# Four of sixteen row tiles of block A's qkv projection are taken out of the projection phase and computed inside block B's attention loop

## The chip, the cores and the metric

The kernel runs on one core of one Trainium2 chip. The metric is the device time of one execution in microseconds (us), and the change is judged by the median over repeated runs. TensorE is called PE here, VectorE DVE, ScalarE ACT, GpSimd POOL and SyncE SP, as in the profile; PEld is PE's loading of weights.

## What is computed

Two attention blocks, A and B, each on an input of 2048 rows and 640 columns with 32 heads of 20 columns. Their outputs stand side by side in the result. All arrays are 32-bit floats.

```python
def _A_ref(x, wqkv, wo):               # W, dil = 8, 2
    q, k, v = qkv[0], qkv[1], qkv[2]   # x @ wqkv, cut into heads
    idx = pos[:, None] - off[None, :]  # 8 positions, 2 apart, backwards
    mask = idx >= 0
    logits = jnp.einsum("bhsd,bhswd->bhsw", q, kg) * scale
    logits = jnp.where(mask[None, None, :, :], logits, -1e9)
    attn = _softmax(logits, axis=-1)
    o = jnp.einsum("bhsw,bhswd->bhsd", attn, vg)
    return (lambda x, *d: x.transpose(*d))(o, 0, 2, 1, 3).reshape(B, S, D) @ wo

def _B_ref(x, wqkv, wo):               # full attention
    scores = jnp.einsum("bhqd,bhkd->bhqk", q, k) * (Dh ** -0.5)
    p = _softmax(scores, axis=-1)
    o = jnp.einsum("bhqk,bhkd->bhqd", p, v)
    return (lambda x, *d: x.transpose(*d))(o, 0, 2, 1, 3).reshape(B, S, D) @ wo
```

## The kernel before

Products of full precision are made from three matmuls: each operand is cut into a rounded part and a remainder (`split`, line 173), and `PASSES` (line 31) names the three pairs of parts that are multiplied. A projection of 128 rows is therefore 5 chunks of the 640 inputs times 3 pairs, that is 15 matmuls into one PSUM bank (`rows15`, line 264; `a_rows`, line 270).

The program has four stretches, each running into the next.

1. **Block A's qkv projection** (lines 515 to 555). Four passes over the 1920 output columns, of 512, 384, 512 and 512 columns (`AC`). In each pass 16 row tiles of 128 rows are projected one after another. ACT copies each tile's PSUM bank into a buffer `ro` (three buffers under the tag `ao`), and SP stores it in DRAM (`a_store`, line 277: `qa_d`, `ka_d`, `va_d`). The weights of the next pass are loaded and split in the middle of a pass (`a_pieces`, line 241).
2. **Block B's q and k projection** (from line 597): 40 groups of 15 matmuls, 512 columns each, stored to `qb_d` and `kb_d`. Block A's attention, which is POOL's work, begins here.
3. **Block B's v projection** (`v_group`, line 926): 32 groups of 15 matmuls of 320 columns, and with them the first 24 steps of the maxima.
4. **Block B's attention loop** (from line 1008), 512 steps. 16 steps make a unit: four heads (a group, 8 in all) times 512 query rows (four to a group), so there are 32 units. A step has two score tiles of two heads each. The exponent needs a row maximum before it, so each score is computed twice: once with the queries along the partitions, for the maximum (DVE, `mx`), and once with the keys along the partitions, for the exponent (ACT, `e`). The maxima run 24 steps ahead of the exponents (`LEAD`). The row maxima go through DRAM (`max_rows`, line 636: `mdr`) and come back as two further rows of the query stack `bq`, so that the score matmul subtracts them.

PE's order in the loop is written out by hand. `UNIT` (near line 847) is the table of one unit, and `b_units` (line 853) walks it. Its entries are: `P`, a step of probabilities times values (16 to a unit, eight matmuls in groups of 32 columns); `ss`, two score matmuls for ACT, in two PSUM banks; `MM`, two matmuls for maxima, reduced together by one DVE instruction over 1024 columns; `sm`, one of each, whose maximum is a DVE instruction over 512 columns; and `G`, which is block A's output projection for half a row tile (`a_out`, line 504), together with the small DVE instructions that have been put aside (`flush`). PSUM has eight banks, and `one` and `two` (lines 142 and 148) choose the bank that will be free first by a running estimate. `UNIT` holds 16 `P`, 18 `ss`, 18 `MM`, 28 `sm` and one `G`.

In this loop POOL does block A's attention (`a_attention`, line 446), paced at one piece in four steps, and adds up the outputs (`braw`). SP issues all transfers in program order. In the first unit of each group it loads the keys, queries and values of the next group (`b_pieces`, line 563): the key stack `bk` is one tile and the query stack `bq` another, of four quarters, out of a pool of four large tiles with the tag `big`. Before the loop the same four hold the columns of x.

In the trace the two kinds of matmuls are told apart by their operands: `ps_st<-bq,bk` with 62 rows is a score for ACT, `ps_st<-bk,bq` with 60 rows a score for a maximum, `ps_st<-e,vb` probabilities times values, `ps_st<-ww,aot` block A's output projection. Nearly all instructions carry line 60, that of the helper which emits them.

Of the kernel before, what the change touches and what calls it, by code (L numbers as in the profile page):

```python
# [40 lines left out]
NKB = 16  # L41
NS = NG * NQC * NKB
# [22 lines left out]
def attention_pair(ctx, tc, xa, wqk_a, wv_a, wo_a, xb, wqk_b, wv_b, wo_b, oa, ob):  # L65
# [98 lines left out]
    va_d = dr.tile([2, PAD + HS, D], F32, name="va_d")  # L164
    qb_d = dr.tile([4, 2 * DH, H, 512], F32, name="qb_d")
# [21 lines left out]
    def columns(n):  # L187

        return (sb.tile([128, 2, KC - 1, 512], F32R, tag="big", bufs=4, name="xn"),
                sb.tile([128, 2, 1, 512], F32R, tag=f"last{n % 4 // 2}", bufs=2, name="xl"))  # L190
# [4 lines left out]
    def x_pieces(x, n, second=None):  # L195

        t = columns(n)
# [106 lines left out]
    XA = [columns(0)]  # L304
# [5 lines left out]
    t, more = x_pieces(xa, 1)  # L310
# [5 lines left out]
    loads = []  # L316
    for n in (2, 3):
        t, more = x_pieces(xa, n)
        XA.append(t)
        loads += more  # L320
# [29 lines left out]
    def a_fetch(n):  # L350
        if n >= len(UNITS):
            return
        t, c = UNITS[n]
        hf, r0 = divmod(t * 128, HS)
# [166 lines left out]
    for k in range(KC):  # L521
        for c in PASSES:
            for t in range(4):
                a_rows(first[t], XA[0], 0, t, W, (k,), (c,))
    for n in range(NA):
        nxt = None
        for t in range(NT):
# [7 lines left out]
            if loads and (n == 0 or t % 2):  # L535
                loads.pop(0)()
            if n == 0 and t == 12:
# [5 lines left out]
            if n + 1 < NA and t == (6 if n == 0 else 2):  # L543
                nxt, loads = a_pieces(n + 1)
            if n == NA - 1:
# [4 lines left out]
                if t % 4 == 0 and t:  # L550
                    w, more = x_pieces(xb, t // 4 - 1)
                    XB.append(w)
# [8 lines left out]
    stacks = {}  # L561

    def b_pieces(g):
        k = sb.tile([128, 2, S], F32R, tag="big", bufs=4, name="bk")
        q = sb.tile([128, NQC, 2, 512], F32R, tag="big", bufs=4, name="bq")
        v = sb.tile([128, NKB, VG], F32, tag="vb", bufs=2, name="vb")
        stacks[g] = (q, k, v)
        out = []
        hs = [slice(g * GH + 2 * r, g * GH + 2 * r + 2) for r in range(2)]

        def add(t, src, runs):
            for r0, s0, n in runs:
                out.append(lambda: sp.dma_start(t[r0:r0 + n].bitcast(F32), src[s0:s0 + n]))
        for r in range(2):
            for r0, s0, n in BK_RUNS:
                add(k[r * HALF:], kb_d[:, hs[r]], [(r0, s0, n)])
        for qc in range(NQC):
            for r in range(2):
                for r0, s0, n in BQ_RUNS:
                    add(q[r * HALF:, qc], qb_d[qc, :, hs[r]], [(r0, s0, n)])  # L580
        return out[:4], out[4:]

    def v_piece(g, b0, b1):

        sp.dma_start(stacks[g][2][:, b0:b1], vb_d[b0 * 128:b1 * 128, g * GH * VC:g * GH * VC + VG]
# [9 lines left out]
    for m in range(0, 10, 2):  # L595
        nxt = []
        for n in range(4):
            for j in range(2):
# [25 lines left out]
                if m == 8 and n > 1:  # L624
                    if (n, j) == (2, 0):
                        k_loads, q_loads = b_pieces(0)
# [81 lines left out]
    def m_matmul(i, j, r, p):  # L708
# [3 lines left out]
        q, k, v = stacks[g]  # L712
# [7 lines left out]
    def max_end(i, n=2):  # L720
# [3 lines left out]
        if left_m[u] == 0:  # L724
            max_rows(*mxt[u], stacks[u // NQC][0], u % NQC)
# [15 lines left out]
    def s_matmul(i, pl, r, p):  # L741
        u, kb = divmod(i, NKB)
        g, qc = divmod(u, NQC)
        q, k, v = stacks[g]
# [26 lines left out]
    def b_pv(i):  # L771
# [15 lines left out]
        for j in range(GH):  # L787
            pe.matmul(acc[32 * j:32 * j + 32, :], stacks[g][2][:, kb, j * VC:j * VC + 32], P[i][j % 2][:, j // 2],
# [21 lines left out]
    def b_two(what):  # L810
# [39 lines left out]
        "MM sm ss P MM MM ss P ss MM sm sm").split()  # L850
    SLOT = UNIT[:UNIT.index("G")].count("P") - 1

    def b_units(pv, group):
# [5 lines left out]
        for i in range(0, NS - LEAD, NKB):  # L859
            for t in UNIT if i + NKB <= NS - LEAD else PAIR * (NKB // 4):  # L860
# [3 lines left out]
                elif t == "G":  # L864
                    group()
                elif t == "ss":
# [20 lines left out]
    def out_first(qc):  # L887

        o = columns(2)
# [54 lines left out]

    V_GROUPS = [(n, half, s) for n in (2, 3, 0, 1) for half in range(2) for s in range(4 * n, 4 * n + 4)]
# [156 lines left out]
```

## Time and profile before

| What | Value |
|---|---|
| median of 3 runs | 1775.66 us |
| lowest and highest | 1774.33 and 1777.3 us |
| the profiled execution | 1773.91 us |
| its span, from the first to the last instruction | 1772.1 us |
| matmuls | 11,211 |
| block A's projection on PE | 5.3 to 212.2 us |
| block B's q and k projection | 212.2 to 349.0 us |
| block B's v projection | 349.0 to 442.9 us |
| the loop's units 0 to 30, by the first score of each | from 439.5 us on |
| granted clock of PE | 1.00 throughout |

The profile is that of one execution. Its page has the busy time of each engine, the span in 40 slices, the transfer queues, the chain of work that ended last, and the costliest groups of instructions. Two cautions apply. A matmul's end is modelled, so PE counts as busy while its results are on the way. And a duration in a group's row is that of one instruction from start to end; in a train, the next may start a little before the last has ended. In a timeline, the bracket behind a row holds the idle time ahead of it on that engine and what ended it.

### The profile page before, as it was taken

What the parts mean: (1) busy time and instruction counts of PE and PEld (TensorE: products, weight loads), DVE (VectorE), ACT (ScalarE), POOL (GpSimd) and SP (SyncE); (2) the same over time, 40 slices, a digit from 0 to 9 for tenths busy, and PEclk for the clock granted to TensorE, in tenths of its full rate; (3) what the DMA queues carried; (4) which work ended last, traced back from release to release, by engine and by line L of the source; (5) the groups of instructions that cost most, each with busy time, mean ns of one, the idle gap of its engine ahead of it and who ended that gap; (6) DMA issues with size and microseconds to landing.
All of it is one profiled execution on the core that took longest, in us unless ns stands there. A gap on an engine that the chain in (4) does not pass through costs nothing.

```text
span 1772.1 us, 31387 instructions
## 1 busy us (share of the span) xinstructions
PE 1761.4 (99%) x11211; PEld 982.3 (55%) x11211; DVE 1332.0 (75%) x1774; ACT 1325.7 (75%) x2593; POOL 1218.8 (69%) x1072
## 2 busy tenths in 40 slices
PE   9999999999999999999999999999999999999999
PEld 8988888888444444444444444444444444444569
DVE  3100232267999999999999999999999999999400
ACT  4222322222999999999999999999999999998981
POOL 0000058448698988989898898989898898745442
PEclk9999999999999999999999999999999999999999
DMA  6333596876443534364444435353543534222123
GB/s 230 112 98 110 175 309 244 278 227 200 121 123 114 138 103 129 115 164 113 129 114 140 119 97 149 123 144 105 156 129 93 143 103 120 87 63 62 57 70 115
DMA packets 191188, 240.20 MB, mean 136 GB/s; under 512 B 89020, under 2 KB 115260, under 8 KB 190040
## 3 DMA queue, kind: packets, MB, share of 16 engines
q1 hardware_dynamic: 190456, 237.54, 44.7%
q8 instruction: 88, 1.44, 0.3%
q14 instruction: 68, 0.56, 0.1%
q10 hardware_dynamic: 576, 0.66, 0.1%
HBM read 173.21 MB, written 64.91 MB: 134 GB/s over the span
## 4 chain that ended last, share of the span: by engine, by line
PE 86%; DVE 5%; ACT 3%; POOL 3%; DMA 1%; issue 1%; SPq 1%; POOLq 0%; DVEq 0%; ACTq 0%
PE ps_st L60 86%; DVE mx L60 5%; ACT e L60 2%; POOL akv L60 1%; ACT more L60 1%; POOL braw L60 1%; SPq L60 1%; DMA bq<-qb_d 1%; DMA stg<-wv_b 0%; ACT al L60 0%; DMA back<-tr_d 0%; POOL aot L60 0%; DMA tr_d<-turn 0%; POOL al L60 0%; POOL ao L60 0%
## 5 line engine op out<-in xcount | busy, mean ns | idle before, releaser
L60 DVE TENSOR_REDUCE mx<-ps_st 128x2 f32<-128x1024 f32 (+1 forms) x1452 | 1204.3, 901 | 53.6 <-PE ps_st L60 50.6
L60 ACT ACTIVATE e<-ps_st 128x512 f32<-128x512 f32 x2048 | 1062.2, 612 | 54.2 <-PE ps_st L60 41.7
L60 PE MATMUL ps_st<-bq,bk 62*128 62x512 f32 x2048 | 616.9, 445 | 1.4 <-ACT e L60 0.9
L60 PEld LDWEIGHTS ps_st<-bq,bk 62*128 62x128 f32 x2048 | 284.1, 184 | 492.6 <-ACT e L60 372.4
L60 PE MATMUL ps_st<-bk,bq 60*128 60x512 f32 x2048 | 551.4, 434 | 2.6 <-DMA bq<-qb_d 1.0
L60 PE MATMUL ps_st<-e,vb 128*32 128x512 f32 x4096 | 542.9, 604 | 0.2
L60 POOL TENSOR_TENSOR braw<-braw,more 128x512 f32<-128x512 f32 x224 | 288.0, 1286 | 147.9 <-ACT more L60 131.8
L60 POOL TENSOR_TENSOR akv<-akv,aq 128x1280 f32<-128x1280 f32 x64 | 188.2, 2940 | 234.8 <-DMA akv<-ka_d 234.7
L60 POOL TENSOR_TENSOR akv<-akv 128x640 f32<-128x640 f32 (+3 forms) x304 | 281.8, 927 | 23.8
L60 PEld LDWEIGHTS ps_st<-bk,bq 60*128 60x128 f32 x2048 | 257.0, 184 | 53.9 <-ACT e L60 25.2
L60 ACT COPY ro<-ps_st 128x320 f32<-128x320 f32 (+2 forms) x124 | 61.3, 496 | 198.9 <-PE ps_st L60 150.8
L60 PEld LDWEIGHTS ps_st<-e,vb 128*32 128x32 f32 x4096 | 82.0, 108 | 154.4 <-issue 74.1
L60 POOL TENSOR_TENSOR akv<-akv,al 128x1280 f32<-128x1280 f32 x64 | 152.1, 2377 | 0.2
L60 PE MATMUL ps_st<-wc,xn 128*128 128x512 f32 (+1 forms) x576 | 134.0, 378 | 0.0
L60 ACT COPY more<-ps_st 128x512 f32<-128x512 f32 x224 | 132.5, 592 | 1.8 <-PE ps_st L60 1.4
L60 PE MATMUL ps_st<-ww,xn 128*128 128x320 f32 x768 | 125.7, 314 | 0.0
L60 PEld LDWEIGHTS ps_st<-ww,xn 128*128 128x128 f32 x768 | 113.4, 188 | 20.0 <-ACT ve L60 8.4
L60 PEld LDWEIGHTS ps_st<-wc,xn 128*128 128x128 f32 x576 | 106.9, 189 | 17.6
L60 PE MATMUL ps_st<-xn,w 128*128 128x512 f32 x480 | 115.8, 390 | 0.0
L60 PEld LDWEIGHTS ps_st<-xn,w 128*128 128x128 f32 x480 | 90.1, 188 | 19.4
L60 ACT CAST pr<-ps_st 128x512 fp32r<-128x512 f32 x40 | 23.5, 587 | 101.4 <-PE ps_st L60 101.4
L60 DVE TENSOR_TENSOR pr<-ps_st,pr 128x512 fp32r<-128x512 f32 x40 | 27.7, 691 | 91.7 <-ACT pr L60 91.7
(64 smaller groups left out, 985.3 us busy)
## 6 DMA issues: line engine op xcount, KB each, us to landing
akv<-ka_d SPq DMA_DIRECT2D x128, 320.0 KB
akv<-va_d SPq DMA_DIRECT2D x128, 320.0 KB
kb_d<-pr SPq DMA_DIRECT2D x20, 512.0 KB
qb_d<-pr SPq DMA_DIRECT2D x20, 512.0 KB
bk<-kb_d SPq DMA_DIRECT2D x16, 640.0 KB
bq<-qb_d SPq DMA_DIRECT2D x64, 160.0 KB
rb<-s_d SPq DMA_DIRECT2D x128, 64.0 KB
stg<-xb SPq DMA_DIRECT2D x12, 512.0 KB
```

The lines of the kernel that those rows point to most:

```text
L60: return self.tc.keep_in_program_order(op(*a, **k))
```

## The change

`UP = 12`: the projection phase now has 12 row tiles in each of its four passes. The last four row tiles are projected in the loop, 320 columns in each of units 0 to 23 (four tiles times six parts of the 1920 columns).

- At tile 9 of each pass, `a_keep` stores the split weights of the pass in DRAM (`wa_d`, six parts of 1.6 MB).
- In the loop, `a_load` brings one part back into the large tile `big2`, which holds nothing else then (`wx`). `a_more`, called at the new entry `V` of the table, does 15 matmuls of 320 columns, an ACT copy and a store, and has the next `a_load` issued three steps later. At the first part of a row tile, `a_columns` loads the tile's 128 rows of x, which POOL splits.
- Units 0 to 23 use a new table, `UNIT_V`, with 16 `P`, 16 `ss`, 16 `MM`, 32 `sm`, one `G` and one `V`. It has the entry `V` behind its fourth `P`. Units 24 to 31 keep `UNIT`.
- The four large tiles now have fixed homes. The keys alternate between `big0` and `big3`. The queries of all groups share one tile in `big1`, a ring of four quarters: in steps 1, 3, 5 and 7 of each unit (from unit 1) the quarter of the unit three later is loaded into the place of the quarter just finished. The last query chunks' x columns, and those of the output projection at the end, get their homes by a list.
- The first chunk of block B's x is loaded in the last pass but one, since `big0` is free.

```diff
+UP = 12
...
+    wa_d = dr.tile([6, 128, 2, KC, 320], F32, name="wa_d")
...
+    def big(home, shape, name):
+
+        return sb.tile(shape, F32R, tag=f"big{home}", bufs=1, name=name)
...
-        return (sb.tile([128, 2, KC - 1, 512], F32R, tag="big", bufs=4, name="xn"),
+        return (big(n if home is None else home, [128, 2, KC - 1, 512], "xn"),
...
+    def a_keep(g, W):
+
+        c, end = AC[g], AC[g + 1]
+        while c < end:
+            m, c1 = divmod(c, 320)
+            n = min(320 - c1, end - c)
+            for wi in range(2):
+                for half, (a, b) in enumerate(AK):
+                    sp.dma_start(wa_d[m, :, wi, a:b, c1:c1 + n],
+                                 W[wi][half][:, :, c - AC[g]:c - AC[g] + n].bitcast(F32))
+            c += n
...
-        for t in range(NT):
+        for t in range(UP):
...
+            if t == 9:
+                a_keep(n, W)
+            if n == NA - 2 and t == 7:
+                w, more = x_pieces(xb, 0)
+                XB.append(w)
+                loads += more
...
+    def b_keys(g):
+        k = big(3 * (g % 2), [128, 2, S], "bk")
+        stacks[g] = (k, v)
+        return [lambda r=r, r0=r0, s0=s0, n=n: sp.dma_start(
+            k[r * HALF + r0:r * HALF + r0 + n].bitcast(F32), kb_d[s0:s0 + n, g * GH + 2 * r:g * GH + 2 * r + 2])
+            for r in range(2) for r0, s0, n in BK_RUNS]
+
+    def b_queries(g, qc):
+
+        return [lambda r=r, r0=r0, s0=s0, n=n: sp.dma_start(
+            rings[0][r * HALF + r0:r * HALF + r0 + n, qc].bitcast(F32),
+            qb_d[qc, s0:s0 + n, g * GH + 2 * r:g * GH + 2 * r + 2])
+            for r in range(2) for r0, s0, n in BQ_RUNS]
...
+            for t in UNIT_V if i // NKB < 6 * (NT - UP) else UNIT if i + NKB <= NS - LEAD else PAIR * (NKB // 4):
...
+                elif t == "V":
+                    more()
...
+    UNIT_V = (
+        "sm P sm MM ss P sm ss MM sm P ss MM sm P sm sm MM sm V sm ss MM sm P sm MM ss P sm MM sm ss P sm MM "
...
+    rows_a = [(t, m) for t in range(UP, NT) for m in range(6)]
+    xt, wt = [], []
+    in_dram = [UP]
+
+    def a_columns(t):
+
+        u = sb.tile([128, 640], F32, tag="stg", bufs=3, name="stg")
+        raw = u.rearrange("p (k c) -> p k c", c=128)
+        sp.dma_start(raw, xa[:, t * 128:(t + 1) * 128].rearrange("(k p) c -> p k c", p=128))
+        x = (sb.tile([128, 2, KC - 1, 128], F32R, tag="last1", bufs=2, name="xn"),
+             sb.tile([128, 2, 1, 128], F32R, tag="x5", bufs=2, name="xl"))
+
+        def parts():
+            for u, r in zip(x, (raw[:, :KC - 1], raw[:, KC - 1:])):
+                gp.tensor_copy(u[:, 0], r)
+                gp.tensor_tensor(u[:, 1], r, u[:, 0].bitcast(F32), ALU.subtract)
+            xt.append(x)
+        after(5, parts)
+
+    def a_load():
+
+        if not rows_a:
+            return
+        t, m = rows_a[0]
+        if m == 0:
+            a_columns(t)
+        w = big(2, [128, 2, KC, 320], "wx")
+        sp.dma_start(w.bitcast(F32), wa_d[m])
+        wt.append(w)
+
+    def a_more():
+
+        t, m = rows_a.pop(0)
+        if m == 0 and len(xt) > 1:
+            xt.pop(0)
+        x, w = xt[0], wt.pop(0)
+        p = bank()
+        rows15(p, lambda xi, k: chunk(x, xi, k), [w[:, 0], w[:, 1]])
+        hf, r0 = divmod(t * 128, HS)
+        pad = PAD if m > 1 else 0
+        store_rows(p, (qa_d, ka_d, va_d)[m // 2][hf, pad + r0:pad + r0 + 128, m % 2 * 320:m % 2 * 320 + 320])
+        if m == 5:
+            after(2, in_dram.__setitem__, 0, t + 1)
+        after(3, a_load)
...
+        if groups == 26:
+            a_load()
...
-            k_loads, q_loads = b_pieces(g + 1)
-            for n, fn in enumerate(k_loads + q_loads + [lambda g=g + 1: v_piece(g, 0, NKB)]):
+            for n, fn in enumerate(b_keys(g + 1)):
                 after(1 + 2 * n, fn)
+            after(41, v_piece, g + 1, 0, NKB)
+        if i >= NKB and i % NKB in (1, 3, 5, 7) and i // NKB + 3 < NG * NQC:
+            b_queries(*divmod(i // NKB + 3, NQC))[i % NKB // 2]()
```

PE's order in the second unit, at its fourth `P` (`ps_st<-e,vb`), before; `bq,bk` is a score for ACT and `bk,bq` one for DVE:

```order
L60 MATMUL ps_st<-bq,bk 128x512 x2
L60 MATMUL ps_st<-bk,bq 128x512 x2
L60 MATMUL ps_st<-bq,bk 128x512
L60 MATMUL ps_st<-bk,bq 128x512
L60 MATMUL ps_st<-e,vb 32x512 x4
L60 MATMUL ps_st<-bq,bk 128x512
L60 MATMUL ps_st<-bk,bq 128x512 x3
L60 MATMUL ps_st<-bq,bk 128x512 x3
L60 MATMUL ps_st<-bk,bq 128x512
L60 MATMUL ps_st<-bq,bk 128x512
```

The same place now. `wx` are the weight parts from DRAM, `xn` and `xl` the two kinds of parts of the row tile's x:

```order
L61 MATMUL ps_st<-e,vb 32x512 x4
L61 MATMUL ps_st<-bq,bk 128x512
L61 MATMUL ps_st<-bk,bq 128x512
L61 MATMUL ps_st<-bq,bk 128x512
L61 MATMUL ps_st<-bk,bq 128x512 x3
L61 MATMUL ps_st<-bq,bk 128x512
L61 MATMUL ps_st<-bk,bq 128x512
L61 MATMUL ps_st<-wx,xn 128x320 x12
L61 MATMUL ps_st<-wx,xl 128x320 x3
L61 MATMUL ps_st<-bq,bk 128x512
L61 MATMUL ps_st<-bk,bq 128x512
L61 MATMUL ps_st<-bq,bk 128x512 x2
```

The fourth `P` was followed by five pairs and the next `P`; it is now followed by four pairs, three of which are `sm` and one `MM`, then by the 15 matmuls of `V`, and then by further pairs ahead of the next `P`.

SP's order in the second unit of the loop (the one that starts at 480.7 us in the trace of before), from `G` on; `mdr` are the row maxima on their way through DRAM, `akv` block A's keys or values, `tr_d` and `back` the way of block A's output through DRAM:

```order
L60 DMA s_d<-sm 128x16
L60 DMA rb<-s_d 32x512 x4
L60 DMA mdr<-mtr 16x2x32 x4
L60 DMA tr_d<-turn 128x640
L60 DMA akv<-va_d 128x640 x2
L60 DMA bq<-qb_d 20x1024
L60 DMA bq<-mdr 2x1024 x2
L60 DMA bq<-qb_d 40x1024
L60 DMA back<-tr_d 32x20x32 x4
L60 DMA akv<-va_d 128x640 x2
L60 DMA bq<-qb_d 20x1024
L60 DMA ot_b<-braw 20x512 x4
```

The same unit now, from the issue of `wx` on:

```order
L61 DMA wx<-wa_d 128x3200
L61 DMA bq<-qb_d 40x1024
L61 DMA akv<-va_d 128x640 x2
L61 DMA oa<-ro 128x320
L61 DMA s_d<-sm 128x16
L61 DMA rb<-s_d 32x512 x4
L61 DMA mdr<-mtr 16x2x32 x4
L61 DMA tr_d<-turn 128x640
L61 DMA akv<-va_d 128x640 x2
L61 DMA bq<-mdr 2x1024 x2
L61 DMA back<-tr_d 32x20x32 x4
```

The pieces of `bq` from `qb_d` stood between the stores of `mdr` and behind its way back; they now stand ahead of `s_d<-sm`, in the first half of the unit, with `wx` (1.6 MB) among them, six entries ahead of the stores of `mdr`.

69 lines of the change are left out of this document (27 added, 42 removed).

## The prediction

> **What bounds the kernel now.** I read the page first, then the busy time of the engines in chosen stretches, then the timelines of single engines in one unit of the loop.
>
> ```profile
> span 1772.1 us, 31387 instructions
> PE   9999999999999999999999999999999999999999
> PEld 8988888888444444444444444444444444444569
> DVE  3100232267999999999999999999999999999400
> GB/s 230 112 98 110 175 309 244 278 227 200 121 123 114 138 103 129 115 164 113 129 114 140 119 97 149 123 144 105 156 129 93 143 103 120 87 63 62 57 70 115
> ```
>
> PE is marked full in every slice, but this hides two regimes. In the first ten slices PEld is at eight to nine tenths and DVE low; from the eleventh PEld falls to four tenths and DVE is full. The stretches say the same in numbers (columns: length, then PE, PEld, DVE, ACT and POOL busy, clock, transfer share, GB/s); the first three are passes 2, 3 and 4 of block A's projection, the others lie in the loop:
>
> ```profile
> 61.03:102.69 41.66, 41.66 (x242) 41.66 (x240) 3.67 (x8) 10.65 (x24) 0.00 (x0) 1.00 0.35 110
> 102.69:157.46 54.77, 54.77 (x242) 45.09 (x241) 3.46 (x5) 11.87 (x21) 0.00 (x0) 1.00 0.31 100
> 157.46:212.23 54.77, 54.77 (x241) 45.09 (x240) 7.93 (x8) 15.46 (x24) 0.00 (x0) 1.00 0.46 151
> 700.00:800.00 100.00, 99.58 (x685) 43.52 (x683) 97.37 (x131) 93.29 (x185) 89.33 (x78) 1.00 0.47 133
> 900.00:1000.00 100.00, 99.77 (x686) 43.72 (x685) 98.11 (x137) 93.25 (x185) 91.46 (x81) 1.00 0.50 138
> ```
>
> The projection is PE's alone: nothing else is near full, and the chain of waits has one unbroken piece of PE there:
>
> ```profile
> 1.36 344.40 PE ps_st L60 x1564
> ```
>
> In the loop DVE is the fullest, with about 2% idle, ACT has 7% and POOL 9 to 11%. How full PE really is has to be read from a timeline. First two steps without `G` (start, length), and PEld's row for the waits inside them:
>
> ```profile
> 732.92 0.49 PE L60 MATMUL ps_st<-bq,bk 62*128 62x512 f32 x2
> ...
> 733.83 1.07 PE L60 MATMUL ps_st<-e,vb 128*32 128x512 f32 x8
> 734.82 0.50 PE L60 MATMUL ps_st<-bq,bk 62*128 62x512 f32 x1
> ...
> 736.64 1.07 PE L60 MATMUL ps_st<-e,vb 128*32 128x512 f32 x8
> 737.64 0.51 PE L60 MATMUL ps_st<-bq,bk 62*128 62x512 f32 x2
> ```
>
> ```profile
> 735.57 0.18 PEld L60 LDWEIGHTS ps_st<-bq,bk 62*128 62x128 f32 x1 [0.22 <-DVE mx L60]
> ...
> 736.15 0.18 PEld L60 LDWEIGHTS ps_st<-bq,bk 62*128 62x128 f32 x1 [0.32 <-ACT e L60]
> ```
>
> Two steps take 737.64 - 732.92 = 4.72 us. Of these PE waits 0.22 + 0.32 = 0.54 us for banks that DVE and ACT still read. Eight such double steps make a unit, so PE waits about 8 x 0.54 = 4.3 us in a unit, a tenth of it. That is all the room that new work has on PE.
>
> **The change part by part.** What goes: tiles 12 to 15 of each of the four passes. Three passes are of 512 columns and one of 384. By the stretches a tile is 54.77 / 16 = 3.42 us or 41.66 / 16 = 2.60 us. Twelve of the first and four of the second make 41.1 + 10.4 = **51.5 us**, all on the path, since PE runs through. The first pass loses the same four tiles at its end, and I give them the same 3.42 us. A rule of the Trainium skill speaks against this term: "TensorE: Matmul & The Clock Gate", section "Back-to-back issue gap", gives about 131 ns for each 512-column matmul in a sustained stream. By it 15 would take 1.97 us, the sixteen tiles at most 31.5 us, and the forecast below would be some 20 us later. The stretches have 3.42 us, and the measurement decides.
>
> What comes: 24 entries `V`. Their price c, per unit, is the question. What the trace has of the kind is `G`, the same 15 matmuls of 320 columns:
>
> ```profile
> 740.86 2.47 PE L60 MATMUL ps_st<-ww,aot 128*128 128x320 f32 x15
> 743.26 0.50 PE L60 MATMUL ps_st<-bq,bk 62*128 62x512 f32 x1
> ...
> 1535.56 2.47 PE L60 MATMUL ps_st<-ww,aot 128*128 128x320 f32 x15
> ...
> 1575.19 4.64 PE L60 MATMUL ps_st<-ww,aot 128*128 128x320 f32 x30
> 1579.76 0.49 PE L60 MATMUL ps_st<-bq,bk 62*128 62x512 f32 x1
> ...
> 1617.06 4.64 PE L60 MATMUL ps_st<-ww,aot 128*128 128x320 f32 x30
> ```
>
> The upper bound is in these rows. From 1535.56 to 1575.19 a unit with one half tile in `G` takes 39.63 us. From 1575.19 to 1617.06, with two directly behind each other, it takes 41.87 us. The second set holds PE for (1579.76 - 1575.19) - (743.26 - 740.86) = 2.17 us, and the unit grew by 2.24: nothing was hidden. The lower bound comes from DVE's rows, the busiest engine:
>
> ```profile
> L60 DVE TENSOR_REDUCE mx<-ps_st 128x2 f32<-128x1024 f32 x596 | 718.5, 1217 | 27.7 <-PE ps_st L60 26.8
> L60 DVE TENSOR_REDUCE mx<-ps_st 128x1 f32<-128x512 f32 x856 | 553.0, 681 | 25.9 <-PE ps_st L60 23.8
> L60 ACT COPY ro<-ps_st 128x320 f32<-128x320 f32 x60 | 25.6, 427 | 59.6 <-PE ps_st L60 59.5
> ```
>
> `UNIT_V` replaces two reductions of 1024 columns by four of 512: 4 x 0.68 - 2 x 1.22 = 0.29 us. ACT gets one copy of 0.43 us, which its 7% idle (2.7 us in a unit) covers. So c lies between 0.3 and 2.24 us. A gain below 0.3 is excluded, since DVE's work grows and DVE has hardly any idle time to give.
>
> Within that I walk through `V` by how DVE fares at `G`:
>
> ```profile
> 739.56 2.41 DVE L60 TENSOR_REDUCE mx<-ps_st 128x1 f32<-128x512 f32 x3
> 741.89 0.34 DVE L60 RECIPROCAL am<-am 128x32 f32<-128x32 f32 x1
> ...
> 743.83 0.69 DVE L60 TENSOR_REDUCE mx<-ps_st 128x1 f32<-128x512 f32 x1 [0.20 <-PE ps_st L60]
> ```
>
> At `G` the matmuls begin at 740.86. DVE still has 741.97 - 740.86 = 1.1 us of reductions in stock, then the put-aside small instructions, and gets its next reduction at 743.83, that is 2.97 us after PE left. `V` has no small instructions, so 2.97 us of stock would be needed. The new order gives `sm sm MM sm` directly ahead of `V`: 3 x 0.68 + 1.22 = 3.3 us of work, handed over while DVE works off about 1.1 us. The stock is thus some 2.2 us, or up to 3 where DVE was behind already: DVE starves 0 to 0.8 us, say 0.4. Then PE must regain its lead. Its 4.3 us of waits in a unit shrink to about 2.1, so that a bank which is late now costs DVE more often; I put 0.4 us on this. The sum is c = 0.3 + 0.4 + 0.4 = **1.1 us**, half-way between the bounds, and 24 x 1.1 = 26.4 us.
>
> The smaller parts:
> - `a_keep`, 36 stores of split weights, 9.8 MB: SP spends 0.3 to 0.4 us on an issue (row below), so 3 to 5 us in a pass, and the row tiles' stores queue behind. Three buffers `ro` cover three tiles, 10.3 us, and eight banks more. Transfers have room (share 0.31 to 0.46). If that cover fails, PE loses a tile per pass, 13 us. I take 1.5 us, bounds 0 and 13.
> - `a_columns`, four times: two POOL instructions of 512 columns (0.61 and 1.31 us by the rows below) and two smaller, at most 3.8 us together, into POOL's idle 9%, 3.6 us in each unit. Nothing; without that cover 15 us, since `braw` and with it ACT's `more` would be late.
> - The ring of queries: the same 128 pieces and bytes, only moved. A quarter is loaded three units ahead, and a half to one and a half units ahead of its maxima. Nothing; were it late, PE would wait at the first maxima of a unit.
> - The homes of the last tiles: nothing.
>
> ```profile
> 77.39 0.32 SPq L60 DMA_DIRECT2D qa_d<-ro  x1
> 77.75 0.42 SPq L60 DMA_DIRECT2D ka_d<-ro  x1
> L60 POOL TENSOR_TENSOR xn<-stg,xn 128x512 fp32r<-128x512 f32 x16 | 20.9, 1306 | 1.3
> L60 POOL CAST xn<-stg 128x512 fp32r<-128x512 f32 x16 | 9.8, 612 | 10.7 <-DMA stg<-ot_b 10.7
> ```
>
> Sum: -51.5 + 26.4 + 1.5 = -23.6 us. The profiled execution took 1773.9 us (span 1772.1 and 1.8 around it), so it would take 1750.3; the median of the runs is 1775.7, 1.8 above it, and becomes **1752**.
>
> **The rivals.**
>
> *`V` is nearly free.* The stock carries DVE over `V` and PE's waits absorb the rest; c is 0.3 to 0.7, and the time 1733 to 1742. For it: PE waits twice as long in a unit as `V` needs. Against it: `G` costs time although small instructions fill DVE's gap. The Trainium skill, "Trainium Kernel Development and Optimization", section "Performance Expectations", calls matmul busy time a bad metric and the busy share of weight loads a good one; by that the loop's PEld of 43% leaves PE more than half free, and this rival would hold. The timeline has a tenth free, which is why it gets only 17%.
>
> *`V` at its full price.* PE cannot regain its lead between `V` and `G`, and c is 1.5 to 2.24 as in the units with 30 matmuls. The time is 1762 to 1779, the upper end no change. For it: 2.2 us measured. Against: there the 30 stand in one piece and with no stock built up. 16%.
>
> *The maxima come late (slower).* `wx` is 1.64 MB on the queue that also carries the row maxima to DRAM and back. It is issued in step 6, the stores of `mdr` in step 11, five steps or 5 x 39.63 / 16 = 12.4 us later. At the fastest slice, 309 GB/s, it needs 5.3 us; at the loop's 133 GB/s, 12.3. Slack now:
>
> ```profile
> 711.27 2.55 SPq L60 DMA_DIRECT2D bq<-mdr  x2
> 718.83 0.50 PE L60 MATMUL ps_st<-bq,bk 62*128 62x512 f32 x2
> ```
>
> The last issue ends at 713.8 and unit 7's first score (the second row) starts 5.0 us later. If `wx` beside the other transfers gets only 83 GB/s, it takes 19.7 us, the maxima are 7.3 late, 2.3 beyond the slack, and PE stands still at 24 unit starts: 24 x 2.3 = 55 us, time 1807. It decides from 1.0 us per unit on, 18.4 us for `wx`. Against it: the pieces of `bq` no longer stand between the maxima's transfers. 7%. The skill's "DMA: Bandwidth & Descriptors", section "Queues, rings and completion order", has each DMA engine take descriptors in ring order, which is this mechanism; no row here shows the order.
>
> *The projection does not shorten as it should.* The keeps and earlier loads press a pass of 41 us below the transfers' pace: 13 us lost, 1765. 5%.
>
> **How the numbers follow.** The forecast, c from 0.7 to 1.5 (1743 to 1762), has 55%. About 0.2%, 3.6 us, is what a measurement of this kernel can tell from no change. Faster by more: 55 + 17 + 5 + the lower part of full price, 9, is 86%. Same: the upper part, 6%. Slower: the late maxima and 1 for prices beyond 2.24, 8%. The range is 1735 to 1771: below lie some 5%, above some 13.
>
> **What would show it.** Right: block B's first group starts near 161 instead of 212 us; units 0 to 23 last 40.4 to 41.2 us and units 24 to 27 still 39.6; behind `V` DVE idles a few tenths. Wrong: units of 41.9 (full price) or under 40.3 (nearly free); PEld or PE waiting for `bq<-mdr` at unit starts; ACT `ro` or PE waiting on stores in the projection.

## The result and the profile after

The changed kernel takes 1798.74 us (median of 4 runs, 1794.98 to 1803.58), the kernel before beside it 1774.99 (1773.40 to 1777.30). The ratio is 1.0134, 95% interval 1.0107 to 1.0162: it is **slower by 24 us**, where 24 faster was forecast. The profiled execution, which the lines below show, was the slowest of the four at 1803.58 us; its span is 29.7 us longer than before.

The page of the changed kernel, with the share of the chain by engine:

```profile
span 1801.8 us, 32005 instructions
PE   9999999999999999989998998999899999999999
PEld 7988888874444454434444444445354444444569
DVE  3112332779999899979998998999799999999400
GB/s 216 202 208 234 309 255 252 239 197 147 170 168 155 170 147 146 184 132 153 168 174 139 169 154 174 157 161 139 177 140 159 143 108 103 101 68 65 63 70 113
PE 84%; DMA 7%; DVE 5%; SPq 2%; issue 1%; ACT 1%; POOL 1%; DVEq 0%; POOLq 0%; ACTq 0%
```

DVE's row reaches 9 in the tenth slice rather than the eleventh: the projection did get shorter. But from slice 11 to 31, where before every digit of PE and DVE was 9, PE now has four 8s, and DVE an 8 or a 7 at the same four places. PE and DVE stop together about once in four units, and 7% of the chain is DMA. The same stretches as before:

```profile
61.03:102.69 41.66, 41.66 (x207) 37.33 (x206) 4.43 (x9) 10.33 (x22) 0.00 (x0) 1.00 0.54 168
700.00:800.00 100.00, 93.02 (x639) 44.05 (x641) 87.88 (x121) 83.52 (x164) 77.56 (x69) 0.97 0.56 163
900.00:1000.00 100.00, 94.96 (x648) 43.97 (x646) 89.29 (x122) 86.25 (x169) 84.62 (x76) 0.97 0.57 165
```

In the loop DVE is now busy for 88 to 89% (97 to 98 before) and PE for 93 to 95. Block B's first group is on PE at

```profile
161.81 2.49 PE L61 MATMUL ps_st<-xn,w 128*128 128x512 f32 x10
```

and the loop's first score at 390.26 us rather than 439.48, 49.2 earlier. From unit 24's first score to the end both kernels take 378.55 us. So the loss lies in units 0 to 23 alone: 1032.99 us against 954.07, **78.9 more, or 3.29 a unit** against 1.1 forecast. Most of these units last 41.0 to 42.6 us, but the first of each later group (4, 8, 12, 16, 20) 45.7 to 48.1, and unit 0 45.6.

What PE waited for there, first in the changed kernel, then before; and what SP's queue waited for, in the same order:

```profile
PE ps_st L61 <- DMA bq<-mdr: 29.6, 10, 6.6
...
SPq L61 <- DMA s_d<-sm: 81.3, 32, 9.6
...
SPq L61 <- DMA bk<-kb_d: 25.8, 11, 3.6
```

```profile
PE ps_st L60 <- DMA bq<-qb_d: 1.0, 2, 0.6
...
SPq L60 <- DMA s_d<-sm: 38.8, 32, 2.9
...
SPq L60 <- DMA bk<-kb_d: 26.0, 9, 4.4
```

PE stands still for the row maxima's way back, ten times, up to 6.6 us; before it never did. Five of these waits, of 4.2 to 6.6 us, stand at the end of a group's first unit; one of 2.1 us lies ahead of the loop's first score, and the others are under 1 us. Unit 8 (731.41 to 779.51) shows how. SP's issues in it:

```profile
737.97 0.55 SPq L61 DMA_DIRECT2D s_d<-braw  x1
743.32 0.32 SPq L61 DMA_DIRECT2D ka_d<-ro  x1
743.73 0.31 SPq L61 DMA_DIRECT2D bk<-kb_d  x1
...
744.96 0.52 SPq L61 DMA_DIRECT2D wx<-wa_d  x1
745.53 0.37 SPq L61 DMA_DIRECT2D bk<-kb_d  x1
...
751.59 1.57 SPq L61 DMA_DIRECT2D bk<-kb_d  x2
...
761.63 0.34 SPq L61 DMA_DIRECT2D s_d<-sm  x1
772.23 1.71 SPq L61 DMA_DIRECT2D rb<-s_d  x4
774.03 1.79 SPq L61 DMA_DIRECT2D mdr<-mtr  x4
...
776.94 0.56 SPq L61 DMA_DIRECT2D bq<-mdr  x2
```

The chain of waits in that unit has

```profile
745.53 16.04 DMA bk<-kb_d
...
761.63 10.58 DMA s_d<-sm
...
776.94 2.53 DMA bq<-mdr
```

SP first stands some 5 us at `V`'s row store (`ka_d<-ro`, 743.32), because the row isn't made yet; `wx` (1.6 MB) and the keys (four transfers, 2.0 MB together; the expectations below count 1.3) are queued behind it. At 761.63 it issues `s_d<-sm`, the 8 KB of reciprocals for the previous chunk's outputs. DVE had these ready at 758.47, but SP stood until 761.57 for the keys' second transfer (the 16.04 us in the chain), which signals its landing on the semaphore that `s_d<-sm` uses next. SP's next transfer, `rb<-s_d`, reads the 8 KB back, so SP waits until they have landed: **10.58 us**. By the trace's semaphore updates `wx` had landed at 759.30; what lay ahead of the 8 KB was the second half of the keys (1.0 MB) and 1.3 MB of other transfers, and all of it was late because `wx` and SP's stand at the row store had gone before. `mdr<-mtr`, the row maxima, stands behind `rb` in SP's program order and so is issued only at 774.03. The maxima's own way there and back then takes 5.5 us; transfers that have nothing to do with them stand ahead. PE at the start of unit 9:

```profile
779.51 0.79 PE L61 MATMUL ps_st<-bq,bk 62*128 62x512 f32 x1 [6.63 <-DMA bq<-mdr]
...
780.23 1.94 PE L61 MATMUL ps_st<-e,vb 128*32 128x512 f32 x8
```

The eight matmuls of a step take 1.94 us, where they take 1.07 at full clock. The granted clock was 0.50 then (the last section).

### The profile page after: what moved, and what is told of

Read it like the earlier page. It is cut to its first block, busy times and chain, and to the rows that moved or that the text cites. A ratio compares the mean times of both kernels' runs of the same rounds, so it can differ in the third digit from the quotient of the medians.

```text
span 1801.8 us, 32005 instructions
## 1 busy us (share of the span) xinstructions
PE 1760.4 (98%) x11331; PEld 1000.2 (56%) x11331; DVE 1348.5 (75%) x1819; ACT 1333.9 (74%) x2598; POOL 1229.3 (68%) x1088
## 4 chain that ended last, share of the span: by engine, by line
PE 84%; DMA 7%; DVE 5%; SPq 2%; issue 1%; ACT 1%; POOL 1%; DVEq 0%; POOLq 0%; ACTq 0%
PE ps_st L61 84%; DVE mx L61 5%; DMA s_d<-sm 3%; DMA bq<-mdr 3%; SPq L61 2%; DMA bk<-kb_d 1%; ACT e L61 1%; POOL akv L61 0%; DMA mdr<-mtr 0%; DVE am L61 0%; POOL al L61 0%; POOL am L61 0%; POOL mtr L61 0%; ACT ro L61 0%; DVE xl L61 0%
## 5 line engine op out<-in xcount | busy, mean ns | idle before, releaser
L61 DVE TENSOR_REDUCE mx<-ps_st 128x1 f32<-128x512 f32 (+1 forms) x1500 | 1220.3, 879 | 113.8 <-PE ps_st L61 104.5
L61 PE MATMUL ps_st<-bq,bk 62*128 62x512 f32 x2048 | 616.9, 442 | 30.5 <-DMA bq<-mdr 29.6
L61 PEld LDWEIGHTS ps_st<-bq,bk 62*128 62x128 f32 x2048 | 290.4, 185 | 517.9 <-ACT e L61 348.4
L61 PE MATMUL ps_st<-bk,bq 60*128 60x512 f32 x2048 | 558.8, 435 | 0.8 <-issue 0.5
L61 PE MATMUL ps_st<-e,vb 128*32 128x512 f32 x4096 | 548.8, 610 | 3.4 <-ACT e L61 0.3
L61 PEld LDWEIGHTS ps_st<-bk,bq 60*128 60x128 f32 x2048 | 270.8, 185 | 29.0 <-DVE mx L61 9.8
L61 PE MATMUL ps_st<-wc,xn 128*128 128x512 f32 (+1 forms) x432 | 101.5, 380 | 0.1
L61 PEld LDWEIGHTS ps_st<-wc,xn 128*128 128x128 f32 x432 | 79.9, 188 | 14.4 <-ACT xn L61 0.7
```

The lines of the kernel that those rows point to most:

```text
L61: return self.tc.keep_in_program_order(op(*a, **k))
```

## The experiments

**The theory** is that two losses add up: `V`'s own price (DVE runs empty at its train of matmuls, and more small reductions), and the stalls for the row maxima, which come from SP's order (`wx`, keys and `V`'s row store ahead of the sums, the sums ahead of the maxima). **The rivals**: `V` simply costs 3.3 us, since PE has no room; or the volume of the loads and keeps (49 MB more) slows everything, in whatever order. "Loop" is the time of units 0 to 23 in the profiled execution (before 954.07, changed 1032.99).

**The loads without their repetition.** `wx` is loaded once, and all units use this first part.

```
+        if not wt:
             w = big(2, [128, 2, KC, 320], "wx")
...
-        x, w = xt[0], wt.pop(0)
+        x, w = xt[0], wt[0]
```

> The weight part wx is loaded once before the loop and used by all 24 V, so 23 loads of 1.6 MB are left out (the parts that the other V compute are therefore not the reference's); PE's order is unchanged. Queue theory (wx on the transfer engines holds up the row sums' small transfers, SP stands at the next one, and the row maxima behind it come late): the stalls at unit starts go, all units 0 to 23 take about 41.0 to 41.2 us as the undisturbed ones do now, and the time is 1775 - 49 + 24 x 1.4 = 1760 us, 1752 to 1766. PE theory (15 more matmuls leave PE no lead, so that unit starts come late whatever is transferred): no change, 1790 to 1800.

Measured: 1771.94 us, ratio 0.9982 (0.9973 to 0.9992); loop 998.6; PE's wait for the maxima falls from 29.6 to 5.2 us. Without the loads 34 us of the loop go, so `V` in itself doesn't cost 3.3 us. What is left, 44.5 us over before, is more than the forecast had for `V`, and the time lies above the queue theory's range.

**The loads without `V`.** The old table, all loads, no matmuls of `V` (the last tiles' rows are then not projected).

```
-            for t in UNIT_V if i // NKB < 6 * (NT - UP) else UNIT if ...
+            for t in UNIT if ...
...
-        rows15(p, lambda xi, k: chunk(x, xi, k), [w[:, 0], w[:, 1]])
```

> The 15 matmuls, the ACT copy and the new table are left out of the 24 units (the old table is used, and the last four row tiles of block A are not computed; a store of the same size from wx stands for the row's store). All loads of wx stay, one a unit, at the same step. Queue theory: the stalls stay, some 35 to 50 us in the 24 units, and the time is 1775 - 49 + 35 to 50 = 1761 to 1776 us, with the late units again the first of each group. PE theory: without V nothing is late, and the time is 1726 us, up to 1735.

Measured: 1737.59, ratio 0.9791 (0.9776 to 0.9806); loop 961.2, only 7.1 over before. The time lies in neither theory's range. The volume alone does little harm: SP's wait at the sums does grow (63.8 us, 38.8 before), but PE waits for the maxima for 3.3 us only. Loads alone 7, `V` alone 44.5, together 78.9: some 27 us belong to neither. By the later runs they come about only when `V` delays `G` (by about 3 us in a unit) and SP (at the row store), and the loads fill the queue.

**The sums behind the maxima.** The broadcast `rb` three steps later, so that SP doesn't stand at it ahead of `mdr`.

```
-            after(2, bcast)
-            after(4, pool, raw, raw, rb, ALU.mult)
+            after(5, bcast)
+            after(7, pool, raw, raw, rb, ALU.mult)
```

> Only SP's order is changed: the broadcast of the row sums (rb, four transfers that wait for s_d from sm) is issued five steps after G, behind the maxima's way to DRAM and back, not two steps after G and ahead of it; POOL's multiplication by it follows two steps later. Queue theory, with SP's place at rb as the link: most of the stalls go, 30 to 43 us are regained, 1756 to 1769 us. Queue theory, with the transfer engines themselves as the link (the maxima's own small transfers stand behind wx too): little is regained, 1785 to 1797. PE theory: no change, 1795 to 1800.

Measured: 1771.71, ratio 0.9991 (0.9977 to 1.0005); loop 1004.6; PE's wait 9.2 us. Two numbers in the source give 27 us back (1798.74 - 1771.71), with all loads and all of `V` in place, though not quite what was expected. SP's stand at `rb` is one link. The queue itself is another: in unit 8 `mdr<-mtr` is now issued at 760.87, but its first transfer lands 10.9 us later, behind the keys, and PE still waits 3.85 us ahead of unit 9.

**The keys later.** The next group's keys nine steps later.

```
-        if sub == 4 and g + 1 < NG:
+        if sub == 13 and g + 1 < NG:
```

> Only the loads of the next group's keys are moved, from steps 5 to 11 of the first unit of each group to steps 14 to 20, behind the maxima's transfers. If it takes wx and the keys together to make the maxima late: the 46 to 48 us units (the first of each group) fall to 41 to 42.5, about 25 us are regained, 1770 to 1778 us. If wx alone is enough: no change, or the stalls move to the second unit, 1790 to 1800. PE theory: no change.

Measured: 1776.80, ratio 1.0010 (1.0000 to 1.0019); loop 1002.7. That is 22 us back, within the range expected: without the keys ahead of it `s_d<-sm` lands in about 1.5 us in the first units. PE's wait falls to 2.1 us, but units 5 and 13 now last 43.1 and 44.5.

**All three together**: sums and keys later, and `wx` in five pieces, three of them behind the maxima.

```
-        sp.dma_start(w.bitcast(F32), wa_d[m])
+        for n, k in zip(steps, range(KC)):
+            after(n, sp.dma_start, w[:, :, k].bitcast(F32), wa_d[m][:, :, k])
...
-        after(3, a_load)
+        after(2, a_load, (1, 2, 9, 10, 11))
```

> The changed kernel with three things moved on the queue: the broadcast of the reciprocals three steps later, the next group's keys nine steps later, and wx in five pieces of 320 KB of which three go behind the row maxima; nothing is left out. Theory (the two losses are separate: 27 us from SP standing ahead of the row maxima, the rest from V itself): every unit of 0 to 23 takes 41.0 to 41.4 us, the first units of a group too, unit 0 stays near 45.5, and the time is 1762 to 1767 us, 8 to 12 below the kernel before. Rival (the late units come from the volume of the loads, 49 MB more in the same time, and not from their order on the queue): units of 43 us and more stay, and the time stays at 1771 or above.

**`wx` alone behind the maxima**, in one piece.

```
-        after(3, a_load)
+        after(11, a_load)
```

> The changed kernel with one thing moved: the load of wx is issued eleven steps behind V rather than three, which is behind the row maxima of its unit; the keys stay where they are, and nothing is left out. Theory (SP stands at the sums because wx and the keys lie ahead of them on the queue, wx alone being enough in the later units): the units of 42.4 us that are not the first of a group fall to 41.0 to 41.4, the first ones of a group, with 1.3 MB of keys ahead of the maxima still, stay near 42 to 43, and the time is 1768 to 1774 us. Rival (wx has then too little time to land before the next V, some 13 us): TensorE waits at V for wx in most units, units stay at 42.5 or more, and the time is 1785 us or more.

Measured: 1776.57 for all three, ratio 1.0012 (1.0000 to 1.0024), loop 1002.3; and 1818.93 for `wx` last, ratio 1.0238 (1.0210 to 1.0266), loop 1046.8. Both expectations of a gain failed, and `wx` last also failed otherwise than its rival said: PE doesn't wait for `wx`. ACT in unit 6, with `wx` last:

```profile
664.54 0.58 ACT L61 COPY braw<-ps_st 128x512 f32<-128x512 f32 x1 [4.97 <-DMA ot_b<-braw]
```

ACT stands 4.97 us, because its copy needs a buffer `braw` whose small store `ot_b<-braw` lies on the same queue behind `wx`. Such waits sum to 26.9 us in this run. In the version with all three the longest is 2.01 us, in unit 5, behind the moved keys; its time is what the rival of volume said, but the next run has the same volume. The queue has a second small transfer that something waits for; moving the large ones to it only changes the victim.

**Keys left where they were**, sums later, `wx` in pieces.

> The changed kernel with the broadcast of the reciprocals three steps later and wx in five pieces, of which three go behind the row maxima; the keys stay at the start of a group's first unit, which e6_all had moved and where it then lost 1 to 2 us in the second unit to a late wx; nothing is left out. Theory (the late units come from SP standing at the sums behind wx and the keys, and in e6_all from the moved keys lying ahead of the last pieces of wx): no unit of 1 to 22 above 42.0, most at 41.0 to 41.4, and the time is 1762 to 1768 us, 6 to 12 below the kernel before. Rival (whatever the order, 2.9 MB in a group's first unit delays something): first or second units of 42.5 and more stay, and the time is 1771 or above.

Measured: **1767.66, ratio 0.9960 (0.9945 to 0.9974)**: faster than both kernels, than the one before by 0.4%. PE never waits for `mdr`. SP in unit 8 of it (724.95 to 766.08):

```profile
738.90 0.53 SPq L61 DMA_DIRECT2D wx<-wa_d  x1
...
740.22 0.53 SPq L61 DMA_DIRECT2D wx<-wa_d  x1
...
753.71 0.38 SPq L61 DMA_DIRECT2D s_d<-sm  x1
754.18 1.80 SPq L61 DMA_DIRECT2D mdr<-mtr  x4
...
763.37 0.56 SPq L61 DMA_DIRECT2D bq<-mdr  x2
...
764.55 1.99 SPq L61 DMA_DIRECT2D rb<-s_d  x4
```

`mdr` now follows `s_d<-sm` at once. The keys are still ahead of it: in unit 8 the row maxima land only 0.35 us ahead of the next unit's first score, in the other units 1 to 6 us. The loop is 996.2: the stalls were worth 1033.0 - 996.2 = **36.8 us**, and `V` with its surroundings 996.2 - 954.1 = **42.1 us**. By medians the stalls are 31.1 us (1798.74 - 1767.66).

The rest of the runs ask what `V`'s 42.1 us are made of. Units 6 and 7 together, undisturbed (length, then PE, PEld, DVE, ACT, POOL busy), before and in this last version:

```profile
678.99:758.32 79.33, 79.11 (x546) 34.20 (x542) 77.86 (x106) 74.53 (x148) 71.46 (x63) 1.00 0.41 120
```

```profile
642.45:724.95 82.50, 82.08 (x575) 39.23 (x572) 79.14 (x110) 75.96 (x150) 73.59 (x64) 1.00 0.53 159
```

The two units are 3.17 us longer, **1.58 each**. DVE is busier by 79.14 - 77.86 = 1.28, or 0.64 each, and idle for 3.36 rather than 1.47, or 0.95 more each. Most of the 0.95 is at `V`. The bracket has it in unit 6 of the last version:

```profile
654.38 4.15 DVE L61 TENSOR_REDUCE mx<-ps_st 128x1 f32<-128x512 f32 x5 [0.68 <-PE ps_st L61]
```

**`V` with five of its 15 matmuls** (the products with a remainder are left out).

```
-        rows15(p, lambda xi, k: chunk(x, xi, k), [w[:, 0], w[:, 1]])
+        for k in range(KC):
+            pe.matmul(p[:, :320], chunk(x, 0, k), w[:, 0, k], start=(k == 0), stop=(k == KC - 1))
```

> As e6_all, but V has 5 of its 15 matmuls (the products of the low parts and of the low weights are left out, so the projected rows of the last tiles are less exact): 0.8 us of TensorE rather than 2.39. Theory (V's price is TensorE's time beyond what the unit had free, seen as starving of VectorE at V): 1.6 us less per V takes off nearly all of the 1.4 us, units 39.7 to 40.1, and the time is 28 to 36 us below e6_all's. Rival (the price is the other table, with more small maxima, and not the matmuls): units stay at 40.8 or more, and the time falls by 10 us or less against e6_all.

Measured: 1768.96, 7.6 us below all three; ratio 0.9961 (0.9948 to 0.9974). Units 6 and 7:

```profile
641.01:722.69 81.68, 79.54 (x554) 36.31 (x552) 79.12 (x110) 76.20 (x150) 73.46 (x64) 1.00 0.54 160
```

They are still 1.18 us each above before. A train of 0.93 us rather than 2.39 takes off only 0.4, and DVE's idle time at `V` falls from 0.68 to 0.24; DVE's busy time stays where it was. So most of `V` is hidden in this table, and the larger part of the price looks like the table's own (no run has this table without `V`). The next runs try other tables.

**`V` in the old table**, at about the same place (queues as in all three), **near the unit's end**, and **three steps behind `G`** (both with the changed kernel's queues).

```
+        ... P sm MM ss sm V sm P sm MM ss ...
```

```
+        ... P MM MM V ss P ss MM sm sm
```

```
+        ... P sm MM ss P sm MM sm V ss P sm MM ss ...
```

> As e6_all, with the unit's table of the kernel before in units 0 to 23 and V put into it between the last scores and the last pair behind its fourth step, about where the other table has it; nothing is left out. Theory (in an undisturbed unit most of the price is the other table, since with 5 of the 15 matmuls only 0.4 of about 1.5 us went): the undisturbed units are 40.4 to 40.8 us, and the time is 8 to 18 us below e6_all's, about 1763. Rival (the table was written to hold V, and without its cover VectorE and ScalarE starve longer): units of 41.2 or more, and the time is e6_all's or above.

> The changed kernel with only the table of units 0 to 23 changed: that of the kernel before with V near the unit's end, in the last step but one, behind its two pairs of wide maxima; wx, keys and sums are queued by the old rules, and nothing is left out. Theory (V in the unit's first third delays G and with it the sums and the row maxima by 3 us, and puts wx ahead of the sums): the unit's work up to the row maxima stands as in the kernel before, wx follows in the next unit's first steps, no unit waits for the row maxima by more than 1 us, VectorE starves 0.4 to 0.8 us at V, units are 40.2 to 40.9, and the time is 1742 to 1760 us, below the kernel before. Rival (V just ahead of the next unit's start only shifts the wait): V's row store makes SP stand ahead of the row maxima's way back, TensorE waits for them at the start of units, units are 42 or more, and the time is 1795 or more.

> As e14_v_end, but V stands three steps behind G, ahead of the scores of that step: the row maxima's write and way back come while SP has V's row store in its queue. Theory (G isn't delayed and wx comes behind the maxima): units of 40.2 to 41.0 and 1742 to 1762 us, as for e14_v_end. Rival (SP stands at V's row store for up to 5 us, as it does in the changed kernel, just where the row maxima come back): units start 1 us or more late, 41.5 to 43 each, and the time is 1775 to 1800.

Measured: 1796.39, ratio 1.0123 (1.0106 to 1.0140); 1791.97, ratio 1.0100 (1.0085 to 1.0115); 1793.46, ratio 1.0108 (1.0093 to 1.0123). All three expectations of a gain failed. DVE at `V` in the second:

```profile
681.29 4.07 DVE L61 TENSOR_REDUCE mx<-ps_st 128x2 f32<-128x1024 f32 x4
687.77 1.82 DVE L61 TENSOR_REDUCE mx<-ps_st 128x2 f32<-128x1024 f32 x2 [2.40 <-PE ps_st L61]
```

DVE idles for the whole train, 2.4 us, and from unit 1 on each unit lasts 42.3 to 42.6, 2.7 above before: without a stock for DVE `V` is paid in full. The changed table thus pays about 0.9 us (1.58 less the 0.68 at `V`) to bring 2.7 down to 1.58. The same run supports the other half of the theory: with the queues of the changed kernel, but `V` and `wx` behind the row maxima, PE waits for no `mdr` and no group's first unit is late.

**The cover taken along.** The cover is what is queued for DVE ahead of `V`. The changed table's steps in another order, `V`'s behind `G`; then the old table up to `G` and `V`'s step with its cover behind it.

```
+        ... G sm MM ss sm P sm sm sm P ss MM sm P sm sm MM sm V sm ss MM sm P sm ss MM sm P sm MM ss P sm MM ss
```

```
+        ... G sm ss MM sm P ss MM sm P sm sm MM sm V sm ss MM sm P sm MM ss P sm MM ss P sm sm P sm sm
```

> The changed kernel with only the order of the steps of its own table for V changed: the same sixteen steps, V's with its cover and the one ahead of it now three steps behind G; queues by the old rules, nothing is left out. Theory (the cost of V is its train of 2.39 us less what is queued for VectorE ahead of it, wherever it stands, and the place sets only the queue's losses): VectorE starves 0.7 to 0.9 us at V rather than the 2.6 of e15_v_late, no unit waits for its row maxima, units are 41.0 to 41.6, and the time is 1758 to 1768 us. Rival (the cover is lost with the place, or fewer maxima ahead of G make the row maxima late): VectorE starves 1.5 us or more at V or TensorE waits for the row maxima, units of 42 and more, and the time is 1775 or above.

> The changed kernel with only the table of units 0 to 23 changed: up to G that of the kernel before, so that each step's products find their scores ready (in e17_v_late_cover there were too few scores ahead, and TensorE waited for their exponentials); behind G the changed kernel's step for V with its cover and the one ahead of it, and lighter steps after them; queues by the old rules, nothing is left out. Theory (V costs its train less the cover; its place decides the queue's losses): VectorE starves 0.7 to 1.0 us at V, no unit waits for the row maxima, units are 40.9 to 41.6, and the time is 1757 to 1768 us, below the kernel before. Rival (the cover belongs to the whole table and isn't had from the steps around V alone): VectorE starves 1.5 us or more, units of 42 or more, and the time is 1780 or above.

Measured: 1893.86, ratio 1.0669 (1.0651 to 1.0687), and 1813.52, ratio 1.0214 (1.0197 to 1.0231). The first is a fault of my table: there are too few scores ahead of the `P`s, and PE's loads wait for the exponentials of scores just issued:

```profile
690.12 0.14 PEld L61 LDWEIGHTS ps_st<-e,vb 128*32 128x32 f32 x2 [0.34 <-ACT e L61]
```

The second is the clean one:

```profile
687.90 2.42 DVE L61 TENSOR_REDUCE mx<-ps_st 128x1 f32<-128x512 f32 x3 [0.63 <-PE ps_st L61]
690.87 4.00 DVE L61 TENSOR_REDUCE mx<-ps_st 128x1 f32<-128x512 f32 x4 [0.55 <-PE ps_st L61]
...
697.04 1.29 DVE L61 TENSOR_REDUCE mx<-ps_st 128x1 f32<-128x512 f32 x2 [0.44 <-PE ps_st L61]
```

At `V` DVE idles 0.63 us as in the changed table, so the cover does travel with its steps. But the small reductions (`sm`) put ahead of `V` are missing in the light steps behind it, where DVE idles again and again, and most units last 43.1 to 43.3. In this table the cover was borrowed from the steps behind it.

**Two trains.** `V` as eight and seven matmuls, first in a table of its own, three steps apart, then in the changed table, one step apart.

> As e6_all, but V is given in two pieces, eight matmuls and seven, three steps apart, with a table of the unit written for it that has more halves of maxima beside scores; nothing is left out. Theory (what V costs is that VectorE runs empty for 0.75 us in the one long train, besides the 0.3 us of more small reductions): the train halves, VectorE doesn't run empty, units are 40.4 to 40.9, and the time is 6 to 18 us below e6_all's. Rival (TensorE is full by then, and 2.39 us is 2.39 us in one piece or two): units stay within 0.3 us of e6_all's or get longer, and the time is within 6 us of it or above.

> As e16_sums_pieces, with V in two trains of eight and seven matmuls one step apart in the same table (e11_split had them three steps apart in another table, and its VectorE was 1.0 us busier and ran empty in many places); nothing is left out. Theory (VectorE starves because one train is longer than its queue): the starving at V falls from 0.75 us to 0.3 or less in both together, units are 40.5 to 40.9, and the time is 6 to 16 us below e16_sums_pieces. Rival (the bank held between the trains takes from the scores and maxima what the shorter train gives): units of 41.2 or more, and the time is that of e16_sums_pieces or above.

Measured: 1805.27, ratio 1.0167 (1.0145 to 1.0190), and 1790.67, ratio 1.0088 (1.0073 to 1.0103): both worse than one train. In the second most units are 42.0 to 42.4, and DVE idles 1.49 us at the second train in unit 6, which has only `sm MM` ahead of it. A second train needs a cover of its own. How much of the loss is the bank held between them wasn't separated.

## Why the prediction was wrong, step by step

- **What bounds the loop, DVE, with PE's room a tenth**: right in the undisturbed units 6 and 7: DVE is busy for 77.86 of 79.33 us before and for 79.14 of 82.50 in the last version (`e16_sums_pieces`), ACT for 74.53 and 75.96.
- **The projection, -51.5 + 1.5 for the keeps**: right; -49.2 measured at the loop's first score. The rate of 3.42 us a tile held. The 131 ns a matmul of the Trainium skill ("TensorE: Matmul & The Clock Gate", section "Back-to-back issue gap") would have made it 20 us less; the trace has 54.77 us for 240 matmuls, 228 ns each.
- **`V`'s price, 1.1 us**: right mechanism, mis-sized. The floor of small reductions was 0.3, and DVE is 0.64 busier: in two units eight more reductions of 512 columns add 5.6 us and four fewer of 1024 save 4.5, since each takes off only 1.13 of its 1.22 us where it overlaps the next. DVE's starving at `V` was put at 0.4, measured 0.68. The lost lead of PE was put at 0.4, and the rest of DVE's added idle time is 0.95 - 0.68 = 0.27. Together 1.58 or, in 24 units, 37.9 us rather than 26.4. Two edges were not counted: in that version unit 0, which also holds two late groups of block B's projection (before: one), is 45.4 us rather than 41.2, and unit 23, where `UNIT_V` meets `UNIT`, 42.6 rather than 39.5. Beyond the 1.58 these are 2.6 and 1.5, which make 42.0 of the 42.1.
- **No term for the row maxima in the sum**: here the forecast failed, and it cost the sign. The rival "the maxima come late" had the place (`wx` on the row maxima's queue) but 7%, and its condition was wrong: it asked whether `wx` itself would take over 18.4 us. It took 7.2 to 14.3. Its slack was misread too: the 5.0 us run from the end of SP's issue, but the rows land some 2.5 us after an issue; in the trace of before they land 2.1 us ahead of unit 7, and within 1 us of the first score of units 3, 11, 15 and 19. What decided was not weighed there: SP, in program order, waits for the 8 KB of `s_d<-sm` to land ahead of `mdr`, and did so before, 38.8 us in 32 units, hidden by slack. The change made that wait longer (`wx` and the keys ahead of it) and the slack shorter: `V` delays `G`, hence the sums, by 3 us of which the unit's own growth gives back 1.6; and SP stands at `V`'s row store, so `wx` and the keys leave 5 us later and the 8 KB meet the keys' second half. I had counted the transfers that were moved, but not the waits of SP at `V`'s store, nor who is queued behind them.
- The rival put 2.3 us on each of 24 unit starts; PE waited at 10, for 3 us on the mean and up to 6.6, and the clock fell with the long ones.
- In sum: 15.7 us for `V` (42.1 - 26.4), 31.1 for the stalls by medians and 0.8 for the projection make 47.6; forecast and result are 1798.74 - 1752.0 = 46.7 apart. The mis-sized price alone left a gain (1767.66); the stalls made it a loss.
- The Trainium skill's "DMA: Bandwidth & Descriptors", section "Queues, rings and completion order", has descriptors taken in ring order on each DMA engine; the prediction said that no row showed this. In the changed kernel's unit 8 the transfers issued from 743.32 to 761.63 us land in the order of their issue, the 8 KB of `s_d<-sm` last, at 772.21, which agrees with it.

## What to carry to other kernels

On an in-order queue, look for small transfers that are waited for on the queue itself (a store that the next entry reads back): the issuing engine stands there, and everything behind them inherits the landing time of what was issued ahead. Before adding a bulk load, list each small transfer that shares its queue, who waits for it and with what slack; moving the load away from one victim can put it ahead of the next. In these tables a train of matmuls that DVE doesn't read left DVE idle for the train's length less what DVE had in stock (0.63 to 0.68 us with a cover, 2.4 without), and a stock taken from the steps behind it was lost there again.

## What the runs showed of the hardware

The granted clock falls with a long stall of PE. The changed kernel around the start of unit 9, which PE reaches at 779.51, and behind the start of unit 13 (the column ahead of the last two is the clock):

```profile
775.98:779.50 3.52, 0.00 (x0) 0.00 (x0) 0.00 (x0) 0.00 (x0) 3.52 (x3) 0.50 0.66 209
779.51:782.81 3.30, 3.30 (x14) 1.10 (x16) 0.69 (x1) 0.60 (x1) 3.15 (x2) 0.50 0.85 279
782.81:786.00 3.19, 3.16 (x26) 1.16 (x26) 2.96 (x4) 3.07 (x7) 2.95 (x5) 1.00 0.72 230
...
950.80:956.00 5.20, 5.16 (x24) 1.51 (x24) 2.40 (x3) 2.08 (x4) 4.81 (x7) 0.50 0.73 237
```

The clock is halved within the wait of 6.63 us and stays so for 3.3 us behind it, in which PE has 14 matmuls; in the next 3.2 us, at full clock, it has 26. So a stall costs more than its length. Inside the loop PE's waits sum to 27.5 us (29.6 less the 2.1 ahead of its first score), the stalls to 36.8. In units 1 to 23 PE is busy at half clock for 21.8 us; at most half of that, 10.9 us, is lost by it, an estimate that would cover the difference of 9.3.

The Trainium skill, "TensorE: Matmul & The Clock Gate", section "Part 1: The HAM clock gate", has the clock at half rate after an idle window of about 3.4 us, until it has been busy for as long. The trace's stretches at 0.50 last 3.4 or 6.8 us and agree with it. But the clock also fell at the wait of 2.1 us ahead of the loop's first score, with PE busy for 1.31 of the 3.41 us before the fall; there the measurement goes beyond the page. With the sums behind the maxima it did not fall at a wait of 2.63 us, ahead of unit 5. The forecast, which had no stalls, left the clock out.
